# Four small edits in the second half of a gated pair of linear-attention blocks: order of row sums, PSUM banks, the queue of one load, and a load in four parts

## The chip, the cores and the metric

The kernel runs on one core of a Trainium2 chip. The metric is the device time of one execution in microseconds, as the median of several runs. The profile is of one further execution of the same program, and its times count from the start of its span. The engines are named as in the profile: PE is TensorE's matrix products, PEld its weight loads, DVE is VectorE, ACT is ScalarE, POOL is GpSimd, and SP is SyncE, which only issues transfers and waits for semaphores.

## The reference

Two linear-attention blocks, A and B, read the same input `x` (2048 rows of 640) with their own weights, and a gate of one number per row mixes their outputs:

```
g = sigmoid((x * gate_w).sum(-1))                # one number per row
q, k, v = split(x @ wqkv)                        # 32 heads of 20 columns each
pq, pk = phi(q), phi(k)                          # phi(t) = t + 1 if t > 0 else exp(t), + 1e-6
kv  = pk^T v (per head, 20 x 20);  z = sum of pk over the rows
o   = (pq kv) / (pq z + 1e-6)
a   = o @ wo                                     # the same for b with B's weights
out = g * a + (1 - g) * b
```

Inputs and output are bf16. The order of summation over rows allows the products to be regrouped: the kernel never forms v. It forms G = x^T pk, then kv = wv^T G with everything outside the heads masked to zero, and M = kv wo, a matrix of 640 x 640 for each block. The output is then pq_A M_A + pq_B M_B, where pq of each block is first scaled, row by row and head by head, by the gate's factor over the normalizer.

## The kernel before, in words

**Layout.** Rows of `x` are handled in 16 tiles of 128. `xn` holds x with rows on the partitions, `xT` holds it transposed (640 = 5 x 128 features on the partitions), `pk` holds phi(k) by rows and `pqT[0]`, `pqT[1]` hold phi(q) of A and B transposed. G lies in two column halves `GT[0]` and `GT[1]`, and `M[0]`, `M[1]` are the two matrices M. A few big products (q, G and the last one) are cut into halves and done with seven products in place of eight, with sums and differences of the halves prepared by VectorE.

**Order.** The kernel is written inside `tc.manual_schedule()`, so every engine does its instructions in the order in which the Python code issues them. Between engines there are semaphores: each engine counts its finished instructions, and transfers take turns on eight semaphores, DMAHW0 to DMAHW7, in the order of their issue in the program. An instruction waits until the counts that it needs are reached, and whatever stands behind it on the same engine waits with it. At the end SP waits in five instructions, two counts each: DMAHW3 and 2, 4 and 1, 5 and 0, 6 and VectorE, 7 and ScalarE. Then comes a drain and the closing barrier of the engines.

**PSUM.** The eight banks are handed out in pools by stage. `ps(name, slot)` gives a pair of banks with the name `ps<slot>`; a tile on a bank waits for the last reader of what lay there before, also across stages. In the stage "weave" the order of allocation puts `ps3` on banks 0 and 1, `ps2` on 2 and 3, and the four cells `q0` to `q3` on 4 to 7. In the stage "after" slot 0 lies on banks 0 and 1, slot 1 on 2 and 3, slot 3 on 4 and 5, and slot 2, in a pool of its own (`hold2`), on 6 and 7.

**Stages around the change** (times of the profiled execution):

- Up to 117 us, "weave": B's phi(k) chunk by chunk, woven with B's phi(q). The last steps there are a chunk of k in slot 2 (its reader on VectorE writes `pk`) and the lifts on ScalarE that read the cells q2 and q3. In the middle, at 82.8 us, SP issues the load of B's value weights, `wv[1]` (`load_w`, called in `Masks.__init__`), one transfer of 800 KB whose first use is at 137.8 us.
- From 114.7 us, "after": `g_pass` forms the last fifth of B's G in 32 products; after the first 16 of them it calls `m_a` three times. `m_a(g, slot)` forms a block of 120 rows of M_A (two products of 320 columns, L656), ScalarE copies it to SBUF (L672) and SP stores it to the DRAM scratch `m_rows` (L665). Two more `m_a` follow, and a sixth inside `g_strassen`, which forms the rest of B's G with seven products, z (`z_rows`) and the normalizer. The slots of the six blocks are 2, 1, 3, then 2, 3, then 2. M_A is read back with another row order (L552).
- 137 to 144 us: kv of B in `kv_mm` and `kv_mask`, then the six blocks of M_B by `m_b`: products on PE, copies on ScalarE and VectorE into `MBr`, and six stores to `m_rows` on SP. `m_load(g0, g1)` (L683 to L688) reads back two blocks at a time into 48, 48 and 32 partitions of `M[1]`; SP issues the three loads behind the last store, each after the two stores that it reads have landed.
- 141 to 182 us, the output stage. A `Pair` i makes row tiles i and i + 8. Its products are p1 and p5 (A's pq with M_A and a difference TM0, done ahead for all or some pairs), p2 (pq of B with the lower half of M_B), p7, p6, p4 (with the differences TM2, TM1, TM3) and p3 (with the upper half of M_B). They accumulate in the banks x, y, z and w, two of each for even and odd pairs. ScalarE copies partial results (`u` of L837, `osb` of L823, the way back L816), VectorE adds them (L779: first `u`, the sum of bank y and ScalarE's copy, then the output tiles `osb`) and SP stores the output; the last pair's second tile goes out on ScalarE's queue in two parts.

The matrices that p2 to p7 need are made by VectorE: `m_sum(2)`, `m_sum(1)`, `m_sum(3)` make TM2, TM1 and TM3 from `M[1]`, which means that they wait for the three loads, and `p_sums(rows, ks)` makes sums of the pq halves, 256 rows at a time. `part[0]` are the rows of pairs 0 and 1, `part[1]` those of pairs 2 and 3. `p_sums` of `part[0]` stands ahead of the M sums, and the sums 2 and 4 of `part[1]` (two instructions, written to `xT`) stand behind them:

```
        for k in (2, 1, 3):
            m_sum(k)
        p_sums(part[1], (2, 4))
        for p in pairs[0:2]:
            p.p2()
            p.c11()
```

`p4` of a pair writes over bank y, so PE's first product of p4 waits until VectorE's `u` of that pair has read y.

Of the kernel before, what the change touches and what calls it, by code (L numbers as in the profile page):

```python
# [15 lines left out]
S, D, H = 2048, 640, 32  # L16
Dh = D // H
DT = D // P
# [6 lines left out]
NG = 6  # L25
# [8 lines left out]
def kernel(  # L34
# [11 lines left out]
    nc = tc.nc  # L46
# [12 lines left out]
    def new_stage(name):  # L59

        if stage:
            stage.pop().close()
        if name is not None:
            held = ctx.enter_context(ExitStack())
            stage.append(held)
            pools["ps"] = held.enter_context(late_pool(name))
# [20 lines left out]
    def ps(name, slot=None):  # L87

        return banks(ps_raw(name, slot))
# [51 lines left out]
    wq_dram = [A_wqkv.rearrange("(c p) f -> p c f", p=P), B_wqkv.rearrange("(c p) f -> p c f", p=P)]  # L141
# [8 lines left out]
    wv = [None, None]  # L150
# [21 lines left out]
    for n in range(1, NB):  # L172
        for c in range(DT):
            nc.sync.dma_start_transpose(
                out=xT[:, c, n * HB:(n + 1) * HB], in_=x2[n * HB:(n + 1) * HB, c * P:(c + 1) * P]
# [4 lines left out]
    for r in range(4):  # L180
# [3 lines left out]
        out=spread[:].rearrange("p (h t) -> p h t", t=TW), in_=I4[:, :, None].to_broadcast([P, H, TW])  # L184
    )
    nc.gpsimd.memset(maskE[:], 1.0)
    for sign, base in ((1, 0), (-1, Dh - 1)):
        nc.gpsimd.affine_select(
            out=maskE[:], in_=maskE[:], pattern=[[-sign * Dh, K6 // Dh], [0, Dh]],
# [3 lines left out]
    for r in range(4):  # L193
        rows = slice(32 * r, 32 * r + 32)
        for sign, base in ((1, 0), (-1, Dh - 1)):
            nc.gpsimd.affine_select(
                out=E4[rows], in_=E4[rows], pattern=[[sign, D]],
# [61 lines left out]
    class Phi:  # L259

        def __init__(self, dst, src, lifted=False):
            self.dst, self.src, self.lifted = dst, src, lifted
            e = work.tile([P] + list(dst.shape[1:]), BF16, tag="e", name="e", bufs=4)
            self.e = e[:]
            self.parts = parts = [(self.e, dst, src)] if not isinstance(src, list) else [
                (self.e[:, n], dst[:, n], part) for n, part in enumerate(src)]
            for to, lifted_to, part in parts:
                nc.scalar.activation(out=to, in_=part, func=ACT.Exp)  # L268
                if lifted is True:
                    self.lift(lifted_to, part)  # L270
# [206 lines left out]
    def g_pass(b, c, slot, between=None, at=ST // 2):  # L477

        pt = ps(f"g{'AB'[b]}", slot)
        for i in range(ST):  # L480
            if between is not None and i == at:
                between()
            for hf in range(2):
                g_mm(c, i, hf, pt)
        for hf in range(2):
            nc.scalar.copy(out=GT[hf][:, c, :], in_=pt[:, hf, 0:HF])

    def g_mm(c, i, hf, pt):
        nc.tensor.matmul(  # L489
            pt[:, hf, 0:HF], lhsT=xn[:, i, c * P:(c + 1) * P], rhs=pk[:, i, hf * HF:(hf + 1) * HF],  # L490
            start=(i == 0), stop=(i == ST - 1),
        )
# [137 lines left out]
    def kv_mm(b, banks, pieces, cs=range(DT)):  # L630

        for g, f0, f1 in pieces:
            hf = f0 // HF
            at = f0 - (g - g % 4) * K6
            for k, c in enumerate(cs):
                nc.tensor.matmul(
                    banks[g // 4][:K6, at:at + f1 - f0], lhsT=wv[b][:, c, e_rows[g]],
                    rhs=GT[hf][:, c, f0 - hf * HF:f1 - hf * HF], start=(k == 0), stop=(k == DT - 1),
                )
# [12 lines left out]
    def m_block(b, g, banks, to=None):  # L652

        at = f_rows[g].start
        for hf in range(2):
            nc.tensor.matmul(  # L656
                banks[hf][:K6, 0:HF], lhsT=kv6[b][:K6, at:at + K6], rhs=wo_sb[b][:K6, g, hf * HF:(hf + 1) * HF],
                start=True, stop=True,
            )
        if to is None:  # L660
            to = work.tile([P, D], BF16, tag="osb", name="m5", bufs=3)
        return to[:f_rows[g].stop - at]

    def m_store(g, to):
        nc.sync.dma_start(out=m_rows[f_rows[g], :], in_=to)  # L665

    def m_a(g, slot):

        pt = ps("mA", slot)
        to = m_block(0, g, cells(pt), M[0][:, g, :] if g < DT else None)  # L670
        n = to.shape[0]
        nc.scalar.copy(out=to.rearrange("p (b n) -> p b n", b=2), in_=pt[:n, :, 0:HF])  # L672
        m_store(g, to)

    def m_b(g, banks):

        to = m_block(1, g, banks, held["mb"][:, g, :] if g < DT else None)
        n = to.shape[0]
        for hf, copy in enumerate((nc.scalar.copy, nc.scalar.copy if g < 2 else nc.vector.tensor_copy)):
            copy(out=to[:, hf * HF:(hf + 1) * HF], in_=banks[hf][:n, 0:HF])  # L680
        m_store(g, to)

    def m_load(g0, g1):  # L683

        rows = slice(f_rows[g0].start, f_rows[g1 - 1].stop)
        nc.sync.dma_start(
            out=M[1][rows.start // DT:rows.stop // DT], in_=m_rows[rows, :].rearrange("(p m) d -> p m d", m=DT)
        )  # L688

    def cells(pt):  # L690
        return [pt[:, hf] for hf in range(2)]
# [22 lines left out]
    def add_rows(dst, a, b, op):  # L714
        nc.vector.tensor_tensor(out=dst, in0=a, in1=b, op=op)  # L715
# [6 lines left out]
    def p_sums(rows, ks=(1, 2, 4)):  # L722

        up = slice(SH + rows.start, SH + rows.stop)
        a11, a21, a12, a22 = [pqT[b][:, :, r] for b in range(2) for r in (rows, up)]
        s2, s4 = xT[:, :, rows], xT[:, :, up]
        for k, dst, a, b, op in (
            (1, a21, a21, a22, ALU.add), (2, s2, a21, a11, ALU.subtract), (4, s4, a12, s2, ALU.subtract)
        ):
            if k in ks:  # L730
                add_rows(dst, a, b, op)

    def m_sum(k):

        lo, hi = slice(0, HF), slice(HF, D)
        a, b = M[0], M[1]
        if k == 1:
            add_rows(TM[1][:], b[:, :, hi], TM[0][:], ALU.subtract)
        elif k == 2:
            add_rows(TM[2][:], b[:, :, hi], a[:, :, hi], ALU.subtract)  # L740
        else:
            add_rows(TM[3][:], b[:, :, lo], TM[1][:], ALU.subtract)
# [17 lines left out]
    def scale(b, m):  # L760

        rec = R[:].rearrange("p h j n -> p (h j n)")
        nc.vector.tensor_tensor(out=pqT[b][:, m, :], in0=pqT[b][:, m, :], in1=rec, op=ALU.mult)
# [109 lines left out]
                out_add(self.osb[0][:, HF + lo:HF + hi], dst, self.u2[:, lo:hi])  # L873
            self.store(0, HF if self.last else 0, D)

    def load_w(b, which, eng):
        lo = {"q": 0, "k": D, "v": 2 * D}[which]
        t = wpool.tile([P, DT, D], BF16, tag="w" + which, name=f"w{which}{'AB'[b]}")
        eng.dma_start(out=t[:], in_=wq_dram[b][:, :, lo:lo + D])
        return t  # L880

    def load_wo(b, eng):
# [68 lines left out]
    def bank(pool, name, n=1):  # L951
        return pool.tile([P, HB] if n == 1 else [P, n, HB], FP32, tag=name, name=name)

    with tc.manual_schedule():
# [11 lines left out]
        for n in range(1, NB):  # L966
            nc.sync.dma_start(
                out=xn[:, n * CB:(n + 1) * CB, :], in_=x2[n * HB:(n + 1) * HB, :].rearrange("(q p) d -> p q d", p=P)
            )
        wv[0] = load_w(0, "v", nc.sync)  # L970
        load_wo(0, nc.sync)
        new_stage("joint")
# [4 lines left out]
            With(chunk(0, ST - 3, 2), ahead=lambda: x_sum(1, 0, 4)), With(chunk(0, ST - 2, 3, True), ahead=lambda: x_sum(1, 4, 8)), With(chunk(0, ST - 1, 2, True), gate_rows, lambda: k_sum(0, 3), lambda: x_sum(2, 0, 4)),  # L977
            With(unit(DT - 1, 3), lambda: k_sum(0, 2))])
        wk[1] = load_w(1, "k", nc.sync)
        held["g"] = ps("gA", 2)  # L980

# [12 lines left out]
        def gated():  # L994
# [3 lines left out]
        q_strassen(0, 1, 1, quad, [With(g_part(0, 10)), With(g_part(10, 12), held["unit"].top, ahead=held["unit"].clamp), With(gated, lambda: k_sum(0, 4)),  # L998
            With(lambda: None)], True)
        wq[1] = load_w(1, "q", nc.sync)  # L1000
        new_stage("mid")
        pts = [ps(f"mid{n}", n) for n in (3, 0, 1)]
# [24 lines left out]
        class Masks:  # L1027

            def __init__(self, slot):
                self.pt = ps("kvA", slot)  # L1030
                kv_mm(0, cells(self.pt), pieces)
                wv[1] = load_w(1, "v", nc.sync)

            def clamp(self):
                kv_mask(0, cells(self.pt), 0, 4)
# [22 lines left out]
        hold = ExitStack()  # L1058
        pools[2] = hold.enter_context(tc.tile_pool(name="hold2", bufs=1, space=bass.MemoryType.PSUM, reuse_waits="tile", side="right"))
        new_stage("after")  # L1060
        g_pass(1, DT - 1, 0, lambda: [m_a(g, slot) for g, slot in enumerate((2, 1, 3))])
        m_a(3, 2)
        m_a(4, 3)
        part = [slice(n * RB, (n + 1) * RB) for n in range(4)]
        held["mb"] = wpool.tile([P, DT, D], BF16, tag="wk", name="MBr")

# [11 lines left out]
        t = wpool.tile([P, 2, DT, HF], BF16, tag="wq", name="TM12")  # L1078
# [14 lines left out]
        pairs[4].p1(None, (2, 3, 4))  # L1093
        m_b(4, acc["z"])
        m_b(5, acc["w"])
        pairs[4].p1_out()
        for g in range(0, NG, 2):
            m_load(g, g + 2)
        scale(1, 4)
        for rows, ks in ((0, (1,)), (1, (1,)), (0, (2, 4))):  # L1100
            p_sums(part[rows], ks)
# [10 lines left out]
        inner = ctx.enter_context(late_pool("inner"))  # L1112
        acc["y"] = [bank(inner, f"oy{n}") for n in range(2)]
        TM[3] = wpool.tile([P, DT, HF], BF16, tag="wk", name="TM3")
        for k in (2, 1, 3):
            m_sum(k)
        p_sums(part[1], (2, 4))
        for p in pairs[0:2]:
            p.p2()
            p.c11()  # L1120
# [58 lines left out]
```

## Time and profile before

| what | value |
|---|---|
| median of 3 runs | 186.67 us (186.53 to 186.91) |
| profiled execution, its own time | 186.59 us |
| its span, first to last instruction | 184.9 us |
| granted TensorE clock | 1.0 throughout |
| PE busy | 179.8 us (97%) |
| DVE busy | 148.4 us (80%) |
| ACT busy | 108.5 us (59%) |
| moved by DMA | 18.00 MB, mean 97 GB/s |

The busy time of an engine is the union of its instructions' spans. Matmuls are pipelined, so PE's 97% does not say that it works at its peak, and holes in its sequence are best seen in the timeline, from the distance of the starts. In the timeline a row is a group of equal instructions: start and duration in microseconds, engine, line, operation, tile written <- tiles read, shape, count, and in brackets the engine's idle time before it with what ended it. A q behind an engine's name (SPq, ACTq) marks its sequencer, which issues transfers and waits. "To landing" is the time from a transfer's issue to its semaphore. L779 and the like are lines of the kernel; where a line is that of a helper, tiles tell the groups apart.

### The profile page before, as it was taken

What the parts mean: (1) busy time and instruction counts of PE and PEld (TensorE: products, weight loads), DVE (VectorE), ACT (ScalarE), POOL (GpSimd) and SP (SyncE); (2) the same over time, 40 slices, a digit from 0 to 9 for tenths busy, and PEclk for the clock granted to TensorE, in tenths of its full rate; (3) what the DMA queues carried; (4) which work ended last, traced back from release to release, by engine and by line L of the source; (5) the groups of instructions that cost most, each with busy time, mean ns of one, the idle gap of its engine ahead of it and who ended that gap; (6) DMA issues with size and microseconds to landing.
All of it is one profiled execution on the core that took longest, in us unless ns stands there. A gap on an engine that the chain in (4) does not pass through costs nothing. (4 is left out here: it accounts for less than half of the span.)

```text
span 184.9 us, 3524 instructions
## 1 busy us (share of the span) xinstructions
PE 179.8 (97%) x1357; PEld 120.8 (65%) x1357; DVE 148.4 (80%) x263; ACT 108.5 (59%) x207; POOL 9.1 (5%) x25
## 2 busy tenths in 40 slices
PE   8999999999999999999999999999999998999993
PEld 3666657665667677676666656767678765777772
DVE  0478989999899799898989897969795959678854
ACT  2065489977883553766777778764715745453210
POOL 8920000000000000000000000000000000000000
PEclk9999999999999999999999999999999999999999
DMA  5995559975018000006000000133912830322132
GB/s 181 298 172 78 108 97 330 331 142 177 0 50 230 17 4 0 0 0 181 2 0 0 4 0 2 51 117 117 253 23 63 217 80 0 128 85 76 71 139 74
DMA packets 20848, 18.00 MB, mean 97 GB/s; under 512 B 9120, under 2 KB 20576, under 8 KB 20832
## 3 DMA queue, kind: packets, MB, share of 16 engines
q1 hardware_dynamic: 19968, 16.97, 34.4%
q10 hardware_dynamic: 864, 0.82, 1.3%
q8 instruction: 10, 0.16, 0.4%
q14 instruction: 6, 0.05, 0.1%
HBM read 11.54 MB, written 4.28 MB: 86 GB/s over the span
## 5 line engine op out<-in xcount | busy, mean ns | idle before, releaser
L299 PEld LDWEIGHTS <-xT 128*128 128x128 bf16 x320 | 31.0, 97 | 15.3 <-issue 0.4
L276 DVE TENSOR_SCALAR e<-e 128x640 bf16<-128x640 bf16 (+2 forms) x58 | 19.7, 341 | 6.3 <-ACT e L268 5.9
L299 PE MATMUL kB<-wkB,xT 128*128 128x320 bf16 x160 | 24.2, 299 | 0.0
L299 PE MATMUL kA<-wkA,xT 128*128 128x320 bf16 (+1 forms) x160 | 23.3, 299 | 0.2 <-DMA wkA<-in_A_wqkv_dram 0.2
L268 ACT ACTIVATE e<-q 128x512 bf16<-128x512 f32 x26 | 15.7, 603 | 5.3 <-PE q L417 4.3
L268 ACT ACTIVATE e<-kA 128x640 bf16<-128x640 f32 x16 | 11.3, 713 | 7.7 <-PE kA L299 7.6
L268 ACT ACTIVATE e<-kB 128x640 bf16<-128x640 f32 x16 | 11.4, 710 | 7.6 <-PE kB L299 7.5
L519 PEld LDWEIGHTS <-xn 128*128 128x128 bf16 x128 | 12.3, 98 | 5.4 <-issue 0.6
L352 PE MATMUL qA<-xT,wqA 128*128 128x512 bf16 x60 | 13.4, 379 | 0.0
L352 PEld LDWEIGHTS <-wqA 128*128 128x128 bf16 x64 | 7.5, 118 | 5.9
L287 DVE SCALAR_TENSOR_TENSOR pk<-kB,e 128x640 bf16<-128x640 f32 x12 | 9.9, 822 | 1.0
L837 ACT COPY u<-ox 128x320 f32<-128x320 f32 x8 | 3.4, 426 | 12.4 <-PE ox L774 12.4
L774 PEld LDWEIGHTS <-pqTB 128*128 128x128 bf16 x80 | 7.7, 98 | 4.1 <-issue 1.2
L774 PEld LDWEIGHTS <-xT 128*128 128x128 bf16 x85 | 8.1, 98 | 2.9
L774 PEld LDWEIGHTS <-pqTA 128*128 128x128 bf16 x85 | 8.0, 98 | 2.9
L779 DVE TENSOR_TENSOR osb<-oz,u 128x320 bf16<-128x320 f32 (+1 forms) x18 | 8.0, 453 | 2.3 <-PE oz L774 1.8
L519 PE MATMUL gs<-pk,xn 128*128 128x320 bf16 x64 | 9.4, 299 | 0.0
L287 DVE SCALAR_TENSOR_TENSOR pk<-kA,e 128x640 bf16<-128x640 f32 x10 | 8.2, 820 | 0.9
L435 DVE TENSOR_TENSOR q<-q,p 128x512 f32<-128x512 f32 x12 | 8.3, 692 | 0.8 <-PE q L417 0.6
L268 ACT ACTIVATE e<-qA 128x1024 bf16<-128x1024 f32 x6 | 6.2, 1028 | 4.2 <-PE qA L352 3.9
L489 PEld LDWEIGHTS <-xn 128*128 128x128 bf16 x64 | 6.2, 98 | 3.1 <-issue 0.3
L519 PEld LDWEIGHTS <-S 128*128 128x128 bf16 x64 | 6.0, 98 | 2.6 <-issue 0.5
(193 smaller groups left out, 358.0 us busy)
## 6 DMA issues: line engine op xcount, KB each, us to landing
out_dram<-osb SPq DMA_DIRECT2D x14, 160.0 KB, 1.8
xn<-in_A_x_dram SPq DMA_DIRECT2D x3, 640.0 KB, 5.2
wvA<-in_A_wqkv_dram SPq DMA_DIRECT2D x1, 800.0 KB
wkB<-in_B_wqkv_dram SPq DMA_DIRECT2D x1, 800.0 KB, 4.7
wqB<-in_B_wqkv_dram SPq DMA_DIRECT2D x1, 800.0 KB
wvB<-in_B_wqkv_dram SPq DMA_DIRECT2D x1, 800.0 KB, 4.9
MA<-m_rows SPq DMA_DIRECT2D x1, 800.0 KB
woA<-in_A_wo_dram SPq DMA_DIRECT2D x1, 750.0 KB
```

The lines of the kernel that those rows point to most:

```text
L268: nc.scalar.activation(out=to, in_=part, func=ACT.Exp)
L276: nc.vector.tensor_scalar(self.e, self.e, 1.0, EPS, op0=ALU.min, op1=ALU.add)
L287: nc.vector.scalar_tensor_tensor(out=dst, in0=src, scalar=1.0 + EPS, in1=e, op0=ALU.add, op1=ALU.max)
L299: nc.tensor.matmul(pt[:, hf, 0:n], lhsT=xT[:, c, i * P:(i + 1) * P], rhs=wk[b][:, c, hf * HF:hf * HF + n], start=(c == 0), stop=(c == DT - 1),
L352: nc.tensor.matmul(dst, lhsT=mixed(wq[b][:, c, :], m), rhs=xT[:, c, n * HB:(n + 1) * HB], start=first, stop=last,)
L435: nc.vector.tensor_tensor(out=dst, in0=src, in1=sb, op=ALU.add)
L489: nc.tensor.matmul(pt[:, hf, 0:HF], lhsT=xn[:, i, c * P:(c + 1) * P], rhs=pk[:, i, hf * HF:(hf + 1) * HF], start=(i == 0), stop=(i == ST - 1),
L519: nc.tensor.matmul(pt[:, n, 0:HF], lhsT=left[:, i, n * P:(n + 1) * P], rhs=right[:, i, :], start=(first and i == 0), stop=(i == hc - 1), s ...
L774: nc.tensor.matmul(dst, lhsT=left[:, c, r0:r0 + P], rhs=right[:, c, :], start=(first and c == 0), stop=(c == DT - 1), skip_group_check=not ...
L779: nc.vector.tensor_tensor(out=dst, in0=acc, in1=sb, op=ALU.add)
L837: nc.scalar.copy(out=self.u2[:], in_=self.at("x"))
```

## The change

Four edits, which do not alter what is computed:

- The sums 2 and 4 of `part[1]` are issued to VectorE ahead of the three sums of M instead of behind them.
- The first five blocks of M_A take the slots 1, 3, 2 and then 3, 2, instead of 2, 1, 3 and then 2, 3.
- The first load of M_B (blocks 0 and 1) is issued on ScalarE's queue, directly behind the copies of the last M_B block and ahead of the copies of p1's results. The other two stay on SP's.
- B's value weights are loaded by four transfers (features 0 to 127, 128 to 255, 256 to 383, and the last 256) instead of one. By the turns of the semaphores, every later transfer then has another semaphore; that of the last store of the output becomes DMAHW7 where it was DMAHW4.

```diff
-    def m_load(g0, g1):
+    def m_load(g0, g1, eng):
 
         rows = slice(f_rows[g0].start, f_rows[g1 - 1].stop)
-        nc.sync.dma_start(
+        eng.dma_start(
             out=M[1][rows.start // DT:rows.stop // DT], in_=m_rows[rows, :].rearrange("(p m) d -> p m d", m=DT)
         )
...
-    def load_w(b, which, eng):
+    def load_w(b, which, eng, cuts=(0, DT)):
         lo = {"q": 0, "k": D, "v": 2 * D}[which]
         t = wpool.tile([P, DT, D], BF16, tag="w" + which, name=f"w{which}{'AB'[b]}")
-        eng.dma_start(out=t[:], in_=wq_dram[b][:, :, lo:lo + D])
+        for c0, c1 in zip(cuts, cuts[1:]):
+            eng.dma_start(out=t[:, c0:c1], in_=wq_dram[b][:, c0:c1, lo:lo + D])
         return t
...
-                wv[1] = load_w(1, "v", nc.sync)
+                wv[1] = load_w(1, "v", nc.sync, (0, 1, 2, 3, DT))
...
-        g_pass(1, DT - 1, 0, lambda: [m_a(g, slot) for g, slot in enumerate((2, 1, 3))])
-        m_a(3, 2)
-        m_a(4, 3)
+        g_pass(1, DT - 1, 0, lambda: [m_a(g, slot) for g, slot in enumerate((1, 3, 2))])
+        m_a(3, 3)
+        m_a(4, 2)
...
+        m_load(0, 2, nc.scalar)
         pairs[4].p1_out()
-        for g in range(0, NG, 2):
-            m_load(g, g + 2)
+        for g in (2, 4):
+            m_load(g, g + 2, nc.sync)
...
+        p_sums(part[1], (2, 4))
         for k in (2, 1, 3):
             m_sum(k)
-        p_sums(part[1], (2, 4))
```

## The prediction

> **What bounds the kernel now.** First the page: which engine is full.
>
> ```profile
> PE 179.8 (97%) x1357; PEld 120.8 (65%) x1357; DVE 148.4 (80%) x263; ACT 108.5 (59%) x207; POOL 9.1 (5%) x25
> ```
>
> TensorE is busy 97% of the span at a granted clock of 1.0 in every slice, so a gain is a hole in PE's sequence that closes, or time after its last matmul. Second, the chain that ended last:
>
> ```profile
> 152.75 0.99 DVE TM L715
> 153.74 0.74 DVE xT L715
> ...
> 154.51 0.82 DVE xT L715
> 155.34 0.41 DVE u L779
> ...
> 155.79 0.84 PE oy L774 x5
> ```
>
> After 155.79 the chain is PE alone up to 181.19. Before it stand four VectorE steps: the last sum of M (TM), two row sums (xT), and u. Third, the timeline of that place:
>
> ```profile
> 147.66 0.82 DVE L715 TENSOR_TENSOR xT<-pqTB,xT 128x1280 bf16<-128x1280 bf16 x1
> 149.30 1.52 PE L774 MATMUL oz<-TM,pqTA 128*128 128x320 bf16 x10
> 150.76 0.99 DVE L715 TENSOR_TENSOR TM<-MB,MA 128x1600 bf16<-128x1600 bf16 x1 [2.27 <-DMA MB<-m_rows]
> 150.78 1.52 PE L774 MATMUL ow<-MB,pqTB 128*128 128x320 bf16 x10
> 153.69 0.43 ACT L837 COPY u<-ox 128x320 f32<-128x320 f32 x1 [0.33 <-PE ox L774]
> 154.17 0.84 PE L774 MATMUL ox<-TM,xT 128*128 128x320 bf16 x5
> 155.25 0.48 DVE L779 TENSOR_TENSOR u<-oy,u 128x320 f32<-128x320 f32 x1
> 155.79 0.84 PE L774 MATMUL oy<-TM,pqTB 128*128 128x320 bf16 x5 [0.78 <-DVE u L779]
> ```
>
> A row of n matmuls of 320 columns starts one every 0.136 us (ten last 1.52 with a last one of 0.30: 1.22/9). So PE was due at 154.17 + 5 x 0.136 = 154.85 and began at 155.79: a hole of 0.94. It was due at 149.30 + 1.36 = 150.66 and began at 150.78, on the last M load: 0.12. VectorE stood idle for 2.27 us just before, for the same load. Fourth, the start of the stage "after":
>
> ```profile
> 114.68 2.34 PE L489 MATMUL gB<-pk,xn 128*128 128x320 bf16 x16
> 115.81 0.82 DVE L287 SCALAR_TENSOR_TENSOR pk<-kB,e 128x640 bf16<-128x640 f32 x1
> 116.28 0.76 ACT L273 ACTIVATE pqTB<-q,lift 128x512 bf16<-128x512 f32 x1
> 117.08 0.97 PE L656 MATMUL mA<-woA,R 120*120 120x320 bf16 x6
> ```
>
> PE was due at 114.68 + 16 x 0.136 = 116.86 and began at 117.08, when ScalarE's lift had ended (117.04): a hole of 0.22. Fifth, SP's rows of the M round trip, with the time to landing of the loads of MB:
>
> ```profile
> 144.29 0.32 SPq L665 DMA_DIRECT2D m_rows<-m  x1
> 144.77 1.72 SPq L686 DMA_DIRECT2D MB<-m_rows  x3
> ```
>
> ```profile
> DMA to landing us min/median/max: 3.8/4.5/4.5
> ```
>
> Three loads go out behind the last store, at 144.77, 145.55 and 146.19, and the last lands at 150.64; both holes near 150.7 end there. Sixth, SP's instructions between 183.89 and 184.10, after the last store has landed:
>
> ```profile
> L1174 SPq EVENT_SEMAPHORE  x3: 28/28/28, 183.9 to 184.0; - x3
> ```
>
> These three do nothing but find their semaphores already there.
>
> **The change, part by part.**
>
> *Row sums.* The two sums of part 1 (xT at 153.66 and 154.51, 1.67 us with their spacing) move from behind the three sums of M to ahead of them. There VectorE is idle from 147.66 + 0.82 = 148.48 to 150.76, so 1.67 fits into 2.28; they read pqT and write columns of xT that no pending product reads, so nothing new is waited for. They are first needed by pair 2. Without them u waits only for its input: ScalarE's copy of ox, ready 153.69 + 0.43 = 154.12, VectorE's last TM ending 153.74. u then runs 154.15 to 154.64 and PE may go on at about 154.69, before it is due at 154.85. The hole of 0.94 closes; ends 0 (another step takes VectorE's place) and 0.94; I take 0.94, since each step that is left has a row, and the margin is 0.16. Next in line is the read of oz0 (done near 155.15, PE needs it at 155.53).
>
> *Banks.* The first three M_A blocks go to slots 1, 3, 2 instead of 2, 1, 3. Slot 2 lies on the banks that ScalarE's last lift reads (to 117.04); slot 1 on the banks of the last kB chunk, free when VectorE's pk step ends at 115.81 + 0.82 = 116.63, before PE is due at 116.86. The block in slot 2 is now third, due at 117.40, after 117.04. The hole of 0.22 closes. Blocks 3 and 4 swap too: block 4 (slot 2, due near 120.1) waits for the third evacuation, which ended 117.55 + 1.88 = 119.43 before; block 5 (122.79) for block 4's, over at 122.2; the z rows for block 3's, earlier than before. From there to 150.66 PE shows no hole above 0.1, and the 0.1 ones are at changes of the matmuls' shape; ScalarE's and VectorE's steps on this stretch begin when PE's products end, and stores and M loads follow them, so all of it moves. The exception is the k sums on VectorE, which end at 122.28 whatever PE does, 0.6 before the z rows (123.16) would need them. Ends 0 and 0.22; I take 0.22.
>
> *First M load on ScalarE's queue.* It waits for stores 0 and 1 alone; store 1 issues at 141.71 and lands 2.1 later, 143.8, when ScalarE ends its last block copy (143.72). Issue, by the two ACT-queue rows, 0.35 (end of the kernel) to 0.46 (start), with 0.1 for its wait: ScalarE goes on near 144.3 instead of 143.62. Behind it stand six copies of p1 products; they had 0.2 idle before each of four, and PE needs the first result at 146.58 (it was done at 144.08) and the sixth at 147.94 (done 147.21). A delay of 0.7 is soaked up there: cost 0; if the wait lasted 1 us more PE would begin to feel it. Gain: load 0 goes out some 0.8 earlier. But loads 1 and 2 keep their times (145.55 and 146.19), because SP waits for stores 2 to 5 to land, and PE needs all three loads. The DMA engines are 80, 84, 90, 101 and 100% busy in the five microseconds from 144, so an earlier start can fill at most 0.2 + 0.16 + 0.1 = 0.46 us: the last landing comes so much sooner at best, or later if load 0 slows the stores. PE can use 0.12 of it. Ends: +0.12 and a loss of 0.6 (load 0's 300 KB, worked at the 240 GB/s of that stretch, 1.2 us, half of it ahead of stores 4 and 5). I take +0.12: the window's empty part is nearest.
>
> [...]
>
> *Value weights in four parts.* Three more issues on SP of 0.39 each (row at 82.81), 1.2 us; SP's next work is at 118.27. The one load of 800 KB landed 4.9 after issue, at 87.7; first use 137.77. Twice that would still be 45 us early: 0. In the products three more weight loads carry a wait that is long met. The first such load already carries one and PE began 137.90 on its beat (136.82 + 8 x 0.136): 0; upper end 3 x 0.1, the hole at 123.16, where a weight load also carries a wait.
>
> *Last store.* Three DMAs more turn the eight semaphores on by three: the last store goes from DMAHW4 to DMAHW7. SP waits at the end in five instructions, for 3 and 2, 4 and 1, 5 and 0, 6 and VectorE, 7 and ScalarE. The last store lands at 182.25 + 1.6 = 183.84; before, three instructions follow the one that it releases (183.92, 183.98, 184.04) and the drain comes at 184.11. With DMAHW7 the first four are done while it flies, and the drain comes near 183.92. Gain 0.19 (ends 0.12 and 0.25).
>
> **Sum.** 0.94 + 0.22 + 0.12 + 0.19 = 1.47. The profiled execution took 186.59 (span 184.9 and 1.7 around it): 185.12, span 183.4. The median of the runs is 186.67, 0.08 above: 185.2.
>
> **Rivals.**
>
> *R1, the load comes late (slower).* Load 0, now on its own queue, takes DMA time from stores 2 to 5, whose landings release loads 1 and 2. For it: the engines are nearly full from 144. Against: the bytes are the same and fill a gap. PE starts 0.14 after the landing, so the whole gain is gone when the last load lands at 150.78 - 0.14 + 0.94 + 0.19 = 151.77, 5.8 us after an unchanged issue near 145.97 (the longest M load took 4.5), and it is slower by 0.37 beyond 152.14. With the 7.9 us of woB, the slowest transfer of that size, it lands at 153.9: 188.8. Range 187.05 to 188.8. [...]
>
> *R2, the wait changes its owner.* PE still stops near 154.85, for ScalarE's copy or for u, because the margin is only 0.16, or at a later sum. For it: u needs PE's product, a copy and an add in a row, and the traces know each at 0.43 to 0.49 only in the old order. Half of 0.94 is lost: 185.7; range 185.5 to 186.2.
>
> *R3, only the tail is won.* The holes close, but what follows (VectorE's adds, which PE meets at 178.96 with a hole of 0.07) gives them back: 186.67 - 0.19 = 186.5. Against: VectorE idles 0.5 to 0.9 before most adds after 158.
>
> **Chances.** Sum as worked 0.68 (its own range 185.0 to 185.5: 0.12 less or 0.3 of weight waits, or 0.15 more); R2 0.17; R3 and other no-changes 0.07; R1 0.08. Measurement tells about 0.2%, 0.37 us, from no change: faster below 186.3, 0.85; same 0.07; slower above 187.04, 0.08. The range 184.95 to 186.2 holds the first two cases.
>
> **What would show it.** Sums: VectorE runs xT, xT, TM, TM, TM from about 148.3 and no idle above 0.6 remains ahead of TM; PE's row oy has no idle. Banks: the first mA follows gB on its beat. Load: ACT's queue issues MB near 143.6 to 144.0; all three landed by 150.4; if ow<-MB stands idle before it, R1. Tail: one semaphore instruction, not four, after the last landing. Wrong if PE has a new hole between 117 and 156, or if the M loads take over 5 us.

## The result, and the profile after

The changed kernel takes 185.75 us (median of 6 runs, 185.63 to 185.94); the kernel before, with more runs beside it, 186.81 (6 runs, 186.53 to 187.38). The ratio is 0.9942, 95% interval 0.9929 to 0.9954: faster by 1.06 us where 1.47 was forecast. The profiled execution took 185.64 us, its span 183.9, at a granted clock of 1.0.

The page of the changed kernel, busy time by engine:

```profile
PE 179.7 (98%) x1357; PEld 121.0 (66%) x1357; DVE 149.0 (81%) x263; ACT 108.4 (59%) x207; POOL 9.1 (5%) x25
```

The work is the same and so are the busy times; only holes can have gone. The timeline of the place where VectorE stood on the path (start, duration, engine, line, operation, tile written <- tiles read):

```profile
148.10 0.82 DVE L715 TENSOR_TENSOR xT<-pqTA 128x1280 bf16<-128x1280 bf16 x1
148.95 0.82 DVE L715 TENSOR_TENSOR xT<-pqTB,xT 128x1280 bf16<-128x1280 bf16 x1
148.99 1.52 PE L774 MATMUL oz<-TM,pqTA 128*128 128x320 bf16 x10
150.94 0.99 DVE L715 TENSOR_TENSOR TM<-MB,MA 128x1600 bf16<-128x1600 bf16 x1 [1.16 <-DMA MB<-m_rows]
150.95 1.52 PE L774 MATMUL ow<-MB,pqTB 128*128 128x320 bf16 x10 [0.44 <-DMA MB<-m_rows]
...
154.32 0.49 DVE L779 TENSOR_TENSOR u<-oy,u 128x320 f32<-128x320 f32 x1 [0.41 <-ACT u L837]
154.34 0.84 PE L774 MATMUL ox<-TM,xT 128*128 128x320 bf16 x5
...
155.02 0.84 PE L774 MATMUL oy<-TM,pqTB 128*128 128x320 bf16 x5
```

The two row sums (xT) run while VectorE waits for the last M load. `u` follows ScalarE's copy instead of a sum, ends at 154.81, and the row `oy<-TM,pqTB` begins 0.68 after the row before it, that is on its beat (5 x 0.136). The hole of 0.94 is gone. But the row `ow<-MB,pqTB` was due at 148.99 + 10 x 0.136 = 150.35 and begins at 150.95: the hole there has grown from 0.12 to 0.60. The start of the stage "after":

```profile
114.60 2.34 PE L489 MATMUL gB<-pk,xn 128*128 128x320 bf16 x16
115.73 0.82 DVE L287 SCALAR_TENSOR_TENSOR pk<-kB,e 128x640 bf16<-128x640 f32 x1
116.19 0.76 ACT L273 ACTIVATE pqTB<-q,lift 128x512 bf16<-128x512 f32 x1
116.77 0.98 PE L656 MATMUL mA<-woA,R 120*120 120x320 bf16 x6
```

The first mA was due at 114.60 + 16 x 0.136 = 116.77 and begins there, while ScalarE's lift still runs until 116.95. The hole of 0.22 is gone. Now the chain of waits around the M round trip (start, duration, what):

```profile
144.03 4.16 DMA m_rows<-m
...
148.28 2.54 DMA MB<-m_rows
150.82 0.14 issue
150.95 1.52 PE ow L774 x10
```

This is what the new hole consists of. The last store of M_B (`m`, 50 KB) is issued at 144.03, its semaphore comes 4.16 us later, SP waits for it, and only then the third M load goes out, at 148.28 instead of 146.19. Before, the store issued at 142.73 landed 2.0 after issue, and the last one, issued at 144.29, at most 1.9 after, since the third load went out at 146.19. The second load kept its time: it was issued 4.53 after the first store of M_B, before 4.50. SP's and ScalarE's rows for the loads, by the tile MB:

```profile
L686 SPq DMA_DIRECT2D MB<-m_rows x2: 307/310/314, 145.3 to 148.3; - x2
L686 ACTq DMA_DIRECT2D MB<-m_rows x1: 380/380/380, 143.5 to 143.5; - x1
```

And the queues in the half microsecond from 145.5, while load 0 moves (q1 is SP's queue, q10 ScalarE's):

```profile
DMA packets 35, 0.17 MB, mean 330 GB/s; under 512 B 6, under 2 KB 10, under 8 KB 35
...
q10 hardware_dynamic: 28, 0.16, 95.4%
q1 hardware_dynamic: 7, 0.01, 4.0%
```

Load 0's queue has 28 packets of it and the stores' queue 7. By the sizes of the packets in the trace, three on each queue are of 4 bytes; the others are 25 rows of the load, of 6400 bytes, and 4 rows of the stores, of 1280. The end of the kernel, SP's instructions between the last landing (183.07) and the drain:

```profile
L1176 SPq EVENT_SEMAPHORE  x1: 28/28/28, 183.1 to 183.1; - x1
```

One in place of four. From the last store's issue to the drain it is 1.66 us, before 1.85.

The holes add up. I call "the stage" the time from the first gB product (114.6) to the drain: 69.43 us before, 68.56 after, 0.87 less. The sum of the terms as measured is 0.94 + 0.23 - 0.48 + 0.19 = 0.88. The rest of the difference between the two profiled executions (186.59 - 185.64 = 0.95) is 0.08 by which the stage began earlier. What lies ahead of the stage is not touched by any kernel here, but differs from one execution to the next: its first product begins between 114.59 and 115.31 in the fourteen profiles. When A's first k weights land near 8 us has a part in it: in `e1_again` a row of kA waits 0.67 for them and begins at 8.73, in the changed kernel PE runs on from 7.76 without a wait. So below I compare stages and holes of the profiles, and name the times beside them.

### The profile page after: what moved, and what is told of

It is laid out like the page before. It is cut to its first block, busy times and chain, and to the rows that moved or that the text cites. A ratio compares the mean times of both kernels' runs of the same rounds, so it can differ in the third digit from the quotient of the medians.

```text
span 183.9 us, 3530 instructions
## 1 busy us (share of the span) xinstructions
PE 179.7 (98%) x1357; PEld 121.0 (66%) x1357; DVE 149.0 (81%) x263; ACT 108.4 (59%) x207; POOL 9.1 (5%) x25
## 4 chain that ended last, share of the span: by engine, by line
PE 91%; DMA 4%; DVE 2%; ACT 1%; issue 0%; SPq 0%; DVEq 0%
PE gs L519 17%; PE kB L299 12%; PE q L417 11%; PE kA L299 11%; PE qA L352 7%; PE oy L774 6%; PE oz L774 4%; PE ox L774 3%; PE ow L774 3%; PE q L352 3%; PE gA L489 2%; PE gB L489 2%; DMA m_rows<-m 2%; PE warm L211 2%; DMA MB<-m_rows 1%; PE qB L352 1%
## 5 line engine op out<-in xcount | busy, mean ns | idle before, releaser
L268 ACT ACTIVATE e<-kA 128x640 bf16<-128x640 f32 x16 | 11.3, 713 | 7.4 <-PE kA L299 7.3
```

## Experiments

The theories at the start: **T1**, load 0 on a second queue takes DMA time from the last stores in proportion to its bytes, the third load goes out late, and that costs the half microsecond; **T2**, the hole before `ow<-MB,pqTB` has another cause than the queue of load 0. Beside them from the start, as T1's rival, stood **T3**, which says that any transfer on a second queue beside this round trip costs, whatever its place and bytes. The misses brought **T4**, which asks why: T4a by two queues moving data at once, T4b because `m_rows` is read while other rows of it are still being written. An expectation of R2 is the prediction's rival of that name.

For each profile the times of the M loads' issues are given from the first store of M_B, all beside these of the kernel before: +3.72, +4.50 and +5.14, hole before `ow` 0.12. The last load has to land by about +9.47 for no hole (PE is due at +9.61 and begins 0.14 after the landing).

**Load 0 back on SP.**

```diff
-        m_load(0, 2, nc.scalar)
         pairs[4].p1_out()
-        for g in (2, 4):
+        for g in range(0, NG, 2):
             m_load(g, g + 2, nc.sync)
```

> The changed kernel with its first M load back on SP's queue, behind the last store, and all else as changed. Theory T1 (load 0 on its own queue takes DMA time from the last stores, so the last store lands after 4.2 us instead of about 1.8, and the last load goes out 2.3 us late): the last load issues near 145.9, lands near 150.35, PE's hole before ow<-MB shrinks from 0.60 to about 0.12, the span falls by 0.48 and the time from 185.75 to about 185.25. Rival T2 (the stores are late because the whole stretch moved: the row sums on VectorE and the earlier products crowd the same memory): the last store still lands late, the hole stays near 0.6 and the time near 185.75.

185.6 us (6 runs), ratio to before 0.9918 (0.9897 to 0.9940). Loads at +3.71, +4.55 and +5.06, hole before `ow` 0.21, stage 68.17, 0.39 less than with the whole change (a hole of 0.12 and 185.25 us were expected). The other three gains stay. The queue of load 0, and with it the time of its issue, is the cause; T2 falls.

**The load's queue alone** (before, with only this edit).

```diff
+        m_load(0, 2, nc.scalar)
         pairs[4].p1_out()
-        for g in range(0, NG, 2):
-            m_load(g, g + 2)
+        for g in (2, 4):
+            m_load(g, g + 2, nc.sync)
```

> The kernel before with one part alone: the first M load on ScalarE's queue. T1: the last store lands some 4 us after its issue, the last load goes out near 148.5 and lands near 151.1 instead of 150.64; the hole before ow<-MB grows from 0.12 to about 0.6, and since VectorE's three sums of M and the two row sums all wait behind that landing, the time rises by about 0.45 to 187.2. T2: nothing is late here, the time stays at 186.7 to 186.8 or falls by 0.1.

187.32 us (12 runs), ratio 1.0009 (0.9995 to 1.0023): no gain, and a loss that the times don't establish. The profile has the mechanism. SP's wait for the last store (in total, times, longest), and SP's loads with the times to landing:

```profile
SPq L686 <- DMA m_rows<-m: 1.9, 1, 1.9
```

```profile
L686 SPq DMA_DIRECT2D MB<-m_rows x2: 307/308/308, 145.5 to 148.3; - x2
DMA to landing us min/median/max: 2.6/3.0/3.4
```

The last store is issued at 144.27 and lands some 3.9 later, and the third load goes out at 148.26, that is +7.24. The hole is 0.33 (0.6 was expected) and the stage 0.22 longer (69.65), half of what was expected. The late load lands in 2.6 us, with no other load beside it for most of that time, where it took 4.45 between the others.

**The row sums alone.**

```diff
+        p_sums(part[1], (2, 4))
         for k in (2, 1, 3):
             m_sum(k)
-        p_sums(part[1], (2, 4))
```

> The kernel before with one part alone: the two row sums ahead of the sums of M. Theory: PE's row of p4 (oy<-TM,pqTB) follows without idle, 0.94 us gained, ratio 0.995; the hole before ow<-MB stays at 0.12 to 0.23. Rival R2 (the wait changes its owner): PE still stops there, for ScalarE's copy or VectorE's u, and half or more of the 0.94 is left as idle.

185.71 us (6 runs), ratio 0.9946 (0.9931 to 0.9961), stage 68.42. Its timeline:

```profile
154.21 0.49 DVE L779 TENSOR_TENSOR u<-oy,u 128x320 f32<-128x320 f32 x1 [0.41 <-ACT u L837]
...
154.23 0.84 PE L774 MATMUL ox<-TM,xT 128*128 128x320 bf16 x5
154.91 0.84 PE L774 MATMUL oy<-TM,pqTB 128*128 128x320 bf16 x5
```

Again 0.68 apart, no hole. The stage is 1.01 shorter: 0.94 and 0.06 by which the hole before `ow` is smaller, which lies within that hole's scatter. One of the four edits gives what the four give together. R2 falls.

**The four-part load alone.**

```diff
-                wv[1] = load_w(1, "v", nc.sync)
+                wv[1] = load_w(1, "v", nc.sync, (0, 1, 2, 3, DT))
```

> The kernel before with one part alone: B's value weights in four parts, by which the last store has DMAHW7. Theory: the drain comes 0.09 us instead of 0.28 after the last landing, no other hole changes, time about 0.19 lower (186.5 against 186.7). Rival (the four loads cost something on the way: SP or the waits on the weight loads): the products of wvB begin late or a hole appears there, and the time does not fall.

186.7 us (12 runs), ratio 0.9991 (0.9975 to 1.0006); 0.19 us is too little for the times to show. The stage is 69.35, as 69.43 less 0.19 and plus 0.11 by which the hole before `ow` was larger. SP's instructions in the profile from 184.15 to 184.25, the last store having landed at 184.16:

```profile
L1175 SPq EVENT_SEMAPHORE  x1: 28/28/28, 184.2 to 184.2; - x1
L1175 SPq DRAIN  x1: 7/7/7, 184.2 to 184.2; - x1
```

Issue to drain is 1.66 as in the changed kernel. In three other kernels of this study (half of load 0, and the two with a foreign load) there is one transfer more, which turns the last store on to DMAHW0, third of the five waits: 1.77. The hole before `ow` was 0.23 with all loads on SP, so its scatter between executions is 0.06 to 0.23.

**Load 0 on ScalarE's queue, later** (behind ScalarE's copy of pair 7's p1, when the last store is on its way).

```diff
-        m_load(0, 2, nc.scalar)
         pairs[4].p1_out()
...
             pairs[k].p1(to)
+            if k == 7:
+                m_load(0, 2, nc.scalar)
```

> As changed, but the first M load goes out on ScalarE's queue later, behind the copy of pair 7's p1 product, near 145.5, when the stores' packets have gone. T1 (it is the meeting with the stores): the last store lands about 2 us after its issue, the last load goes out near 146 and lands near 150.3, the hole before ow<-MB is 0.0 to 0.2, time 185.2 to 185.35. Rival T3 (any load on a second queue costs, since two queues share the engines badly): the last load lands past 150.7, hole above 0.4, time 185.6 or more.

185.88 us (7 runs), ratio 0.9937 (0.9915 to 0.9959). Load 0 goes out at +4.46, and the stores are no longer late, as T1 has it; SP issues at +4.50 and +5.34. But the hole is 0.72 and the stage 68.68: T1's gain did not come. Its chain of waits:

```profile
143.26 2.08 DMA m_rows<-MBr
...
146.25 4.85 DMA MB<-m_rows
151.10 0.14 issue
151.24 1.52 PE ow L774 x10
```

The loads take 4.7 to 5.1 us to landing instead of 3.8 to 4.5. T3's numbers came, but the second queue is not shown to be the reason. Load 0 left 0.74 later than on SP's queue (+3.72), because the edit places it behind a copy of ScalarE, and in between the DMA engines had nothing to move. The 0.7 us behind the stores, here and then, as far from the first store, in the run `e1_again` below with all loads on SP's queue; the last two numbers are the busy share of the DMA engines and GB/s:

```profile
145.50:146.20 0.70, 0.70 (x8) 0.51 (x6) 0.70 (x2) 0.45 (x2) 0.00 (x0) 1.00 0.00 0
```

```profile
145.80:146.50 0.70, 0.70 (x7) 0.51 (x6) 0.70 (x2) 0.45 (x2) 0.00 (x0) 1.00 0.95 159
```

That pause is longer than the 0.53 by which the hole exceeds the 0.19 of the latter, so the late start is enough to explain it; this run does not show T3.

**Half of load 0** (block 0 alone, 24 partitions and 150 KB, on ScalarE's queue, block 1 on SP's).

```diff
-        m_load(0, 2, nc.scalar)
+        m_load(0, 1, nc.scalar)
         pairs[4].p1_out()
+        m_load(1, 2, nc.sync)
         for g in (2, 4):
```

> As changed, but only block 0 (24 partitions, 150 KB) is loaded on ScalarE's queue and block 1 on SP's in the old place: half the bytes that cross the stores. T1 (bytes on the other queue ahead of the last stores set their delay): the last load issues about 1 us late instead of 2.3 (near 6.0 to 6.6 us after the first store's issue, against 5.1 with all on SP and 7.5 as changed), the hole before ow<-MB lies between 0.2 and 0.6. Rival T3 (a second queue as such costs the time): the hole stays at 0.6 or above.

186.01 us (8 runs), ratio 0.9949 (0.9932 to 0.9966), hole 0.93, stage 69.00. With half the bytes the hole lies within the 0.52 to 0.99 that the whole load gave in three profiles. SP's rows in the timeline, and then rows of the chain of waits:

```profile
144.73 1.38 SPq L665 DMA_DIRECT2D m_rows<-m  x1
146.22 1.63 SPq L686 DMA_DIRECT2D MB<-m_rows  x3
```

```profile
144.73 2.75 DMA m_rows<-m
...
147.55 4.31 DMA MB<-m_rows
...
152.00 1.52 PE ow L774 x10
```

SP itself was held for 1.38 us in the issue of the last store (0.27 to 0.32 in the other kernels), and the last three stores landed after 2.75 to 3.04. The last load went out at +6.09, 0.95 late where the whole load made it 2.4 late: the delay did go with the bytes, as T1 has it. The hole did not follow, because three loads were then in flight together, and the last of them took 4.31 where it took 2.54 with the whole load ahead.

**The last store instead of the load on ScalarE's queue** (loads on SP).

```diff
-    def m_store(g, to):
-        nc.sync.dma_start(out=m_rows[f_rows[g], :], in_=to)
+    def m_store(g, to, eng):
+        eng.dma_start(out=m_rows[f_rows[g], :], in_=to)
...
-        m_store(g, to)
+        m_store(g, to, nc.scalar if g == DT else nc.sync)
```

> All three loads on SP's queue, and the last store of M_B (40 rows, 50 KB) on ScalarE's queue instead: this time the small transfer that is waited for is put on the queue of its own. By T1, turned round, it lands early (near 145.3 instead of 146.1), the last load goes out up to 0.5 us sooner, as soon as the store before it has landed, and the hole before ow<-MB falls from 0.2 to 0.0 to 0.15: 0.1 to 0.2 us better than with the loads on SP alone, about 185.3. If store 4 is as late as store 5, nothing is won: hole 0.2.

185.86 us (12 runs), ratio 0.9956 (0.9941 to 0.9971), hole 0.90, stage 68.86. Chain:

```profile
143.93 4.40 DMA m_rows<-m
...
148.43 2.68 DMA MB<-m_rows
```

The picture turned round: with the load on SP's queue and the store on the other, the store is late again, though its issue begins 0.15 ahead of the load's; T1 turned round had it land early. It is not a precedence of ScalarE's queue: both times the store that lands late (4.16 and 4.40) has a load on the other queue beside it. With all on SP's queue, in the profile before, the loads' rows begin when the stores' rows end, near +4.7.

**A foreign load of 300 KB** (all M loads on SP; 48 rows of 6400 bytes of `x` into a tile no longer read).

```diff
         pairs[4].p1_out()
+        nc.scalar.dma_start(out=pk[0:48, 0:5, :], in_=x2[0:240, :].rearrange("(p m) d -> p m d", m=DT))
         for g in range(0, NG, 2):
             m_load(g, g + 2, nc.sync)
```

> The version with all three M loads on SP, plus one load on ScalarE's queue right after the copy of pair 4's p1 product (near +3.9 us after the first MBr store): 300 KB of the input x, 48 rows of 6400 B as in load 0, into a tile whose content is no longer read. Nothing that it moves has to do with m_rows, and nothing waits for it. T4a (two queues that move data at the same time hold each other up, whatever they move): the stores that are in flight then land after 3 to 4 us instead of about 2, the second or third M load is issued at +7 instead of +5.1, and the hole before ow<-MB,pqTB is 0.5 or more. T4b (what hurts is that m_rows is read while other rows of it are still being written): the stores land in about 2 us, the loads go out at +3.7, +4.5 and +5.1, and the hole stays at 0.1 to 0.3, up to 0.6 if the 300 KB only add their bytes to the loads' own time.

One run, 186.36 us. Loads at +3.74, +6.49 and +7.25, hole 1.23, stage 69.30. Chain, and the queues from 144 to 145:

```profile
144.03 3.89 DMA m_rows<-m
...
147.99 3.46 DMA MB<-m_rows
```

```profile
q10 hardware_dynamic: 25, 0.16, 89.9%
q1 hardware_dynamic: 5, 0.00, 1.1%
```

Stores take 3.9 to 4.1 us though nothing of `m_rows` is read by the second queue, and while the foreign load moves 0.16 MB, 25 rows of 6400 bytes, the stores' queue moves three rows of 1280. T4b falls. (The 300 KB also add to what the stretch has to move, so this hole is no price of the queue alone.)

**A foreign load of 10 KB** (16 rows of 640 bytes, same place).

```diff
+        nc.scalar.dma_start(out=pk[0:16, 0, 0:HF], in_=x2[0:16, 0:HF])
```

> The same with a tiny load in the same place: 16 rows of 640 B, 10 KB, of x into the dead tile. If a second queue that has any work holds up the stores, they land late as in the run with 300 KB. If the bytes or the number of large packets count, the stores land in about 2 us, the loads go out at +3.7, +4.5 and +5.1, and the hole before ow<-MB,pqTB is 0.1 to 0.3.

One run, 186.21 us. Loads at +3.73, +4.56 and +5.24, stores after 1.9 to 2.1, stage 68.57. Chain:

```profile
144.60 1.89 DMA m_rows<-m
...
146.56 4.74 DMA MB<-m_rows
```

A second queue as such does not stop the stores: T4a holds for the big load, not for a small one. Three kernels here have a load on ScalarE's queue issued at +2.21, and the landing of the stores behind it grows with its size: 1.9 to 2.1 us with 10 KB, 2.75 to 3.04 with 150 KB (half of load 0), 3.9 to 4.1 with 300 KB. The hole was 0.51, though, because the loads took 4.2 to 4.7 us; with one run that is not told from scatter.

**The two versions once more, side by side**, and the changed kernel in another series.

> The changed kernel with load 0 back on SP, for a direct comparison with the changed kernel on the same chip. T3 and T4: hole before ow<-MB,pqTB 0.1 to 0.3, loads at +3.7, +4.5 and +5.1, median 0.2 to 0.4 us below the changed kernel's, ratio to the kernel before 0.992 to 0.9945. If the load's queue made no difference to the time: equal to the changed kernel within 0.1 us.

> The changed kernel once more beside the last. Hole before ow<-MB,pqTB 0.5 to 0.6, second M load issued beyond +7, ratio to the kernel before 0.994 to 0.996.

> The changed kernel again, in one series with the next ones, since executions in the last series spread by half a microsecond. T1: the last store lands some 4 us after its issue, 2 us later than with all loads on SP's queue, the hole before ow<-MB is 0.5 to 0.6, the ratio to the kernel before 0.994.

With load 0 on SP: 185.63 us (185.38 to 185.83, 6 runs), ratio 0.9945 (0.9929 to 0.9962), hole 0.19, stage 68.15. As changed, same series: 185.89 (185.56 to 186.60, 12 runs), ratio 0.9964 (0.9945 to 0.9983), hole 0.99 (0.5 to 0.6 was expected), third load at +7.85, stage 68.94. In the other series: 185.86 (185.03 to 187.03, 12 runs), ratio 0.9959 (0.9941 to 0.9977), hole 0.52, third load at +7.40, stage 68.47. The chain of the version with load 0 on SP:

```profile
149.60 1.36 PE oz L774 x10
150.96 0.03 issue
150.99 1.52 PE ow L774 x10
```

The round trip has left the chain; PE runs through. Its stage was 68.17 and 68.15 in two profiles, against 68.56, 68.47 and 68.94. In the medians it is ahead by 0.12 to 0.29 us, and the intervals of the ratios overlap: the gain of 0.3 to 0.8 is shown by the profiles, in the times it has the right sign and is not settled to its size. It has the shortest stage of all versions run.

## Why the prediction was right, and where it was not

- **Row sums, 0.94: right.** The hole closed wholly, in the change and alone (stage 1.01 less). The margin of 0.16 for `u` was enough: it ends 0.2 before PE's next row.
- **Banks, 0.22: right.** 0.23 closed in every profile with the new slots, and stayed in the three without.
- **First M load, +0.12: wrong, -0.48.** The step that failed is "loads 1 and 2 keep their times (145.55 and 146.19), because SP waits for stores 2 to 5 to land". The condition was the right one, and I took the landings it names as given. They were what load 0 changed: the last store landed 4.16 after issue instead of at most 1.9, and the third load went out at 148.28; load 1 did keep its time. "The window's empty part is nearest" chose the wrong end; the other end, -0.6, was nearly it (0.60 - 0.12 = 0.48 here; 0.87 in the worst profile of the same kernel, beyond that end). So rival R1's mechanism came to pass, at a price below the gains instead of above them, since the late load landed in 2.54 us. My threshold, a last landing at 151.77, was not reached (150.82). Two of my signs failed with it: the landing by 150.4, and no idle above 0.6 ahead of TM (1.16).
- **What load 0's queue costs.** 0.39 (stage) against the same kernel without it, a loss where I had +0.12. The rows say where it goes: while load 0 or the foreign load moved on the second queue, 25 of its rows went against 4 of the stores in the half microsecond from 145.5, and 25 against 3 in the microsecond from 144, and the last store landed after 4.16 and 3.89 where it took at most 1.9 before.
- **ScalarE's delay, 0: right.** The copies of p1 soaked up the issue: the row `oz<-TM,pqTA` ahead of the hole begins 8.25 after the first store of M_B, before and after.
- **Four parts, 0, and last store, 0.19: right**, as 1.85 to 1.66, in every profile with eight semaphores turned on by three.
- **Sum.** 0.94 + 0.23 + 0.19 = 1.36 of the 1.35 expected from the other three; the load took 0.48 of it. R2 (half of 0.94 lost) fell. R3 fell as well: the gains in the middle arrive at the end of the kernel.
- **Luck in the number.** 185.75 lies outside the 185.0 to 185.5 that I gave to the sum as worked, and next to R2's 185.7, though R2's mechanism did not occur. That the whole range of 184.95 to 186.2 holds it is owed to R2's share of that range, not to the term of the load.
- **Two readings that were off.** The 7.9 us of woB was not the slowest transfer of its size: woA's part of 150 KB took 11.3. And VectorE idles 0.5 or more before seven of its 38 adds after 158, not before most. Neither enters the sum; the first sets R1's upper end, the second argues against R3.

Left open is by what rule a load of 6400-byte packets holds the other queue's 1280-byte packets up. Shown: it is not the address (3.9 to 4.1 beside rows of `x`), and not the order of the two engines' queues (4.16 with the load on ScalarE's, 4.40 with the store there). The delay of the stores goes with the load's size, about 1 us at 150 KB and 2 us at 300 KB, and is none at 10 KB; those 10 KB were in packets of 640 bytes, so at that end the packets' size and the amount are not told apart. Not run is load 0 on SP's own queue ahead of the last two stores, which would part the second queue from the early start.

## What to carry to other kernels

The third load here waited for the landing of stores and had its time set by the slowest of them: it went out at +7.53 with a landing of 4.16, at +5.14 with one of at most 1.9. Before starting something earlier beside such stores, ask what the earlier transfer does to their landing. For this round trip through DRAM, which nearly fits its window (a hole of 0.12 before), one queue in order (0.06 to 0.23 of hole) was better than two, in each placement tried (0.33 to 0.99). A step that an engine does on the path while it stood idle shortly before was the best find of this profile: moving two sums (1.67) by three instructions, into 2.27 of idle time, gave all that the change was worth (stage 1.01 less alone, 0.87 with the other edits).

## What the runs showed of the chip

- A store of this round trip took 1.9 to 2.1 us to its landing with one queue at work (before, `e1_again`), and the last of them, 50 KB, 3.9 to 4.5 while another queue moved a 300 KB load, with SP's queue at 4.0% of the engines' time for half a microsecond in the changed kernel and at 1.1% for a microsecond beside the foreign load. Beside a load of 150 KB it took 2.75, beside one of 10 KB 1.9.
- SP's issue of the last store took 1.38 us instead of 0.27 to 0.32 while half of load 0 was on the other queue.
- The place of the last store's semaphore in the closing waits was worth about 0.06 us for each waiting instruction behind it: 1.85, 1.77 and 1.66 us from the last issue to the drain with three, two and none.
